# Weight chunks loaded out of order into free ring slots and idle projection buffers, new planned costs for three GpSimd operations, and one tail copy moved to ScalarE

## Chip, cores and metric

One core of one Trainium2 chip. The metric is the device time of one execution in microseconds (us), taken over several executions; the profiles are single executions. The chip can slow TensorE's clock; the share of full speed that it allows is called the granted clock here. The experiments ran on four occasions, each on another chip, and each time the kernel before ran along.

## The reference

Two layers, each of attention (32 heads of 16) and a gated feed-forward network, on a sequence of 2048 with width 512 and F = 1792. The second layer uses the same weights again.

```python
def _A_ref(x, wqkv, wo):                      # H = 32, Dh = 16
    qkv = (x @ wqkv).reshape(B, S, 3, H, Dh).transpose(2, 0, 3, 1, 4)
    q, k, v = qkv[0], qkv[1], qkv[2]
    p = softmax(einsum("bhqd,bhkd->bhqk", q, k) * Dh ** -0.5)
    return einsum("bhqk,bhkd->bhqd", p, v).transpose(0, 2, 1, 3).reshape(B, S, D) @ wo

def _B_ref(x, w_gate, w_up, w_down):
    return (gelu(x @ w_gate) * (x @ w_up)) @ w_down

x = x + _A_ref(layernorm(x), wqkv, wo)        # S = 2048, D = 512
x = x + _B_ref(layernorm(x), w_gate, w_up, w_down)
x = x + _A_ref(layernorm(x), wqkv, wo)        # the same two again
x = x + _B_ref(layernorm(x), w_gate, w_up, w_down)
```

## The kernel before

The attention takes nearly all of the time. TensorE forms the scores, ScalarE exponentiates most tiles (VectorE computes the others with integer arithmetic), TensorE multiplies the result by V. The feed-forward network of a block of 512 rows is fitted in between the attention work of the next block, so only the last half-block of the second layer is left for a tail without attention.

How the order of the instructions comes about: the kernel does not write them down in a fixed order. A planner in Python, run while the kernel is built, records them one by one. It keeps its own clock: each recorded operation has a **planned cost**, and each engine a time at which it is next free.

```python
def op(self, eng, fn, r=(), w=(), grp=None, cost=0.1, lat=0.15, at=0.0):
    start = max(self.free[eng], at, self.ready(eng, r, w))
    # ... dependencies on earlier reads and writes ...
    self.free[eng] = start + cost
    o.seen = start + cost + lat
    return o
```

In each step the main loop compares these planned times, and so decides what comes next on TensorE:

```python
while True:
    t = now[0] = max(now[0], sch.free["pe"])
    pump(t)                        # jobs of VectorE, GpSimd, SP whose planned start is before t
    # ...
    F = fill_ready()
    if F is not None and F <= t + 0.02:
        fill()                     # scores for the next exponential
        continue
    # ...
    if fit >= 1 and (full >= want or full and (rest or press)):
        pv(its, min(fit, full, 6)) # attention times V
        continue
    # ... else a piece of projection or feed-forward work that fits before the limit,
    # ... else keep_clock(): a filler matmul of zeros, added to the accumulator bank
    now[0] = t + 0.05
sch.model = (now[0], log["idle"], dict(sch.free))   # the planned end
```

The program that is built gives every engine its instructions in that order, with waits for what they need, whatever the real durations turn out to be.

The last half-block's weights come in 256 KB chunks, in a ring of slots `WR` and, for that half-block only, in six spare slots in the buffers of the projection weights `WK`, `WV`, `WQ`. Chunks are loaded strictly in order, so a chunk that has to wait holds up all behind it; and the spare slots wait until all projection work (`prep`) has been taken off its list:

```python
wst = {"loaded": 0, "next": 0, "here": set(), "done": set()}
# ...
def wfeed():
    while wst["loaded"] < len(wlist):
        i = wst["loaded"]
        if wlast[i] >= 0 and wlast[i] not in wst["done"] or wslots[i] >= NWR and prep:
            break
        wload()
```

The LayerNorm's reciprocal root is three short GpSimd operations; the last argument of each is its planned cost. Most calls have `n` = 2 or 4 columns, those in the tail `n` = 1:

```python
def ln_scale(n, then, lo=0):
    # ...
    job("pool", 1, [
        (lambda e: e.tensor_scalar(LNS[:, 0, lo:lo + n], var, LN_EPS, None, op0=ALU.add), keys,
         [("LNS", lo + i) for i in range(n)], 0.3),
        (lambda e: e.tensor_tensor(LNS[:, 1, lo:lo + n], LNS[:, 0, lo:lo + n], CM05[:, 0:n], op=ALU.pow),
         [("LNS", lo + i) for i in range(n)] + [("CM05",)], [("LNS", lo + i) for i in range(n)], 1.1),
        (lambda e: e.tensor_scalar(LNS[:, 2, lo:lo + n], mean, -1.0, None, op0=ALU.mult),
         keys + [("LNS", lo + i) for i in range(n)], [("LNS", lo + i) for i in range(n)], 0.3)], then)
```

Of the kernel before, what the change touches and what calls it, by code (L numbers as in the profile page):

```python
# [175 lines left out]
def _emit_fast(nc, es, x_in, wqkv, wo, wg, wu, wd, out, n_rep=2):  # L176
# [12 lines left out]
    NCK = D // 128  # L189
# [3 lines left out]
    NQB = S // 512  # L193
# [15 lines left out]
    def sb(name, shape, dt):  # L209
        return es.enter_context(nc.sbuf_tensor(name, shape, dt))  # L210
# [12 lines left out]
    NWR = 7  # L223
# [4 lines left out]
    CM05 = sb("fCM05", [128, 4], F32)  # L228
# [19 lines left out]
    LNS = sb("fLNS", [128, 3, 8], F32)  # L248
# [20 lines left out]
    def bankbf(b):  # L269
        return PS[:, b, :].bitcast(F16)  # L270
# [3 lines left out]
    def dma(eng, grp, dst, src, r=(), w=(), serial=False, kb=32):  # L274
        if grp not in sch.groups:
            sch.add_dma_group(grp, serial=serial)
        t = max(sch.free[eng], sch.ready(eng, r, w)) + 0.5
        wire[0] = max(t, wire[0]) + kb / 180.0
        return sch.op(eng, lambda e: e.dma_start(dst, src), r=r, w=w, grp=grp, cost=0.5, lat=wire[0] - t + 1.3)
# [101 lines left out]
    wlist = []  # L381
    for layer in range(n_rep):
        for qb in range(NQB):
            halves = layer == n_rep - 1 and qb == NQB - 1 and NQB > 1
            for h in ((0, 1) if halves else (None,)):
# [2 lines left out]
                    w_tail = len(wlist)  # L388
                wlist += [("g", i) for i in range(NFT // 2)] + [("u", i) for i in range(NFT // 2)]
                wlist += [("d", i) for i in range(NFT // 2)]  # L390
    wst = {"loaded": 0, "next": 0, "here": set(), "done": set()}
    NWX = 6 if NQB > 1 else 0
    wslots, wlast = [], {}
    for i in range(len(wlist)):
        k = i - w_tail
        s = NWR + k % (NWR + NWX) if 0 <= k and k % (NWR + NWX) < NWX else None
        if s is None:
            s = i % NWR if k < 0 else (w_tail + k - NWX) % NWR
        wslots.append(s)
        wlast[i] = max([j for j in range(i) if wslots[j] == s], default=-1)  # L400

    def wslot(s):
        if s < NWR:
            return WR[:, s, :]
        W = (WK, WV, WQ)[(s - NWR) // 2]
        return W[:].rearrange("p a b -> p (a b)")[:, 2 * D * ((s - NWR) % 2):2 * D * ((s - NWR) % 2 + 1)]

    def wload():
        i = wst["loaded"]
        wst["loaded"] += 1  # L410
        kind, k = wlist[i]
        s = wslots[i]
        if kind == "d":
            dst = wslot(s)[:, 0:2 * D].rearrange("p (a b) -> p a b", a=2)
            src = wd_src[:, 2 * k:2 * k + 2, :]
        else:
            dst = wslot(s)[:, 0:NCK * 256].rearrange("p (a b) -> p a b", a=NCK)
            src = (wg_src if kind == "g" else wu_src)[:, :, 256 * k:256 * (k + 1)]
        keys = [("WR", s)]
        if s >= NWR:  # L420
            keys += [(("WK", "WV", "WQ")[(s - NWR) // 2], c) for c in range(NCK)]
        job("sp", 1, [(lambda: dma("sp", "wr%d" % s, dst, src, w=keys, serial=True, kb=256), [], keys, None)],
            lambda o: wst["here"].add(i))

    def wfeed():
        while wst["loaded"] < len(wlist):
            i = wst["loaded"]
            if wlast[i] >= 0 and wlast[i] not in wst["done"] or wslots[i] >= NWR and prep:
                break
            wload()  # L430

    def wget(kind, k):
        i = wst["next"]
# [4 lines left out]
    def wdone(i):  # L438
        wst["done"].add(i)
        wfeed()  # L440
# [13 lines left out]
    def job(eng, prio, ops, then=None, ported=False):  # L454

        serial[0] += 1
        jobs[eng].append((prio, serial[0], ops, then, ported or eng == "pool"))
# [51 lines left out]
    have = set()  # L509
# [7 lines left out]
    def give_back(b):  # L517
        if b in lent:
            lent.discard(b)
            slot_open[0 if b in SLOTS[0] else 1] -= 1  # L520
        elif b in held3:
            held3.discard(b)
        else:
            free_banks.add(b)
# [35 lines left out]
    def evac_job(prio, b, ops, then=None):  # L560
        def done(o):
            give_back(b)
            if then is not None:
                then(o)
        dve(prio, ops, done)

    def xn(i, alt):
        return HT[:, i + 4 * alt, 0:D].bitcast(F16)

    def xnkey(i, alt):  # L570
        return ("HT", i + 4 * alt)
# [5 lines left out]
    def ln_scale(n, then, lo=0):  # L577
        keys = [("MV", lo + i) for i in range(n)]
        mean = AP(MV, 2 * lo, [[16, 128], [2, n]])
        var = AP(MV, 2 * lo + 1, [[16, 128], [2, n]])  # L580
        job("pool", 1, [
            (lambda e: e.tensor_scalar(LNS[:, 0, lo:lo + n], var, LN_EPS, None, op0=ALU.add), keys,
             [("LNS", lo + i) for i in range(n)], 0.3),
            (lambda e: e.tensor_tensor(LNS[:, 1, lo:lo + n], LNS[:, 0, lo:lo + n], CM05[:, 0:n], op=ALU.pow),
             [("LNS", lo + i) for i in range(n)] + [("CM05",)], [("LNS", lo + i) for i in range(n)], 1.1),
            (lambda e: e.tensor_scalar(LNS[:, 2, lo:lo + n], mean, -1.0, None, op0=ALU.mult),
             keys + [("LNS", lo + i) for i in range(n)], [("LNS", lo + i) for i in range(n)], 0.3)], then)

    def ln_check(n, lo=0):
        var = AP(MV, 2 * lo + 1, [[16, 128], [2, n]])  # L590
        dve(2, [(lambda e: e.scalar_tensor_tensor(OKV[:, 0:n], var, L_HI, OKV[:, 0:n], op0=ALU.is_le, op1=ALU.mult),
                 [("MV", lo + i) for i in range(n)] + [("OKV",)], [("OKV",)], 0.1)])

    def ln_apply(i, rows, key, eng, alt, then=None, us=None, st=0):
        us = us or (1.05 if eng == "pool" else 0.46)
        job(eng, 1, [(lambda e: e.tensor_scalar(xn(i, alt), rows, LNS[:, 2, st + i:st + i + 1], LNS[:, 1, st + i:st + i + 1],
                                                op0=ALU.add, op1=ALU.mult),
                      [key, ("LNS", st + i)], [xnkey(i, alt)], us)], then, ported=True)

    def transpose_piece(i, tt, alt=False, eng="dve", then=None):  # L600
        def fn(e, bs):
            for ck in range(NCK):
                ins = e.transpose(bankbf(bs[0])[:, ck * 128:(ck + 1) * 128], xn(i, alt)[:, ck * 128:(ck + 1) * 128],
                                  IDN[:, :])
            return ins

        def after(bs):
            b = bs[0]
            dst = XNT[:, :, tt * 128:(tt + 1) * 128]
            src = bankbf(b)[:, 0:NCK * 128].rearrange("p (a b) -> p a b", a=NCK)  # L610
            if eng == "act":
                sch.op("act", lambda e: e.activation(dst, src, ACTF.Copy), r=[BK[b]], w=[("XNT", tt)], cost=0.6)
                give_back(b)
                if then is not None:
                    then(None)
            else:
                evac_job(1, b, [(lambda e: e.tensor_copy(dst, src), [BK[b]], [("XNT", tt)], 0.335)], then)

        return Piece(0.06 * NCK, [xnkey(i, alt), ("IDN",)], fn, after)
# [14 lines left out]
    def got(name):  # L634
        return lambda o: have.add(name)
# [179 lines left out]
    prep = []  # L815
# [175 lines left out]
    def ln_thread(tts, xsl, check, name, eng, step=2):  # L991

        nt = len(tts)

        def scale(lo):
            hi = min(lo + step, nt)

            def apply(o):
                for i in range(lo, hi):
                    ln_apply(i, X[:, xsl[i], :], ("X", xsl[i]), eng, False, got(("xn", name, i)))  # L1000
            ln_scale(hi - lo, apply, lo)
            if check:
                ln_check(hi - lo, lo)

        ready = 0
        for i, tt in enumerate(tts):
            while ("xn", name, i) not in have:
                while ready < nt and all(("st", name, k) in have for k in range(ready, min(ready + step, nt))):
                    scale(ready)
                    ready += step  # L1010
                yield None
            yield transpose_piece(i, tt, then=got(("tr", name, i)))
        while not all(("tr", name, i) in have for i in range(len(tts))):
            yield None

    def post(layer, qb, h):
# [13 lines left out]
        for i, tt in enumerate(tts):  # L1030
            def evac_x(b, i=i, x=xsl[i]):
# [4 lines left out]
                           [("AT", c, k) for c in range(NCK) for k in hs]  # L1036
                           + [("WO",)], evac_x, cols=D)
        yield from ln_thread(tts, xsl, True, (layer, qb, 2, h), "dve" if qb == NQB - 1 else "pool",
                             1 if h == 1 else 2)
        xs = slice(512 * qb + q0, 512 * qb + q0 + qn)  # L1040
# [171 lines left out]
    unit_order = []  # L1212
# [97 lines left out]
    def left():  # L1310
        return cur or nxt[0] < len(segs)
# [327 lines left out]
    while True:  # L1639
# [62 lines left out]
        now[0] = t + 0.05  # L1702
        log["idle"] += 0.05
        assert now[0] < 20000.0, "no progress"
    assert not unit_order and wst["next"] == len(wlist) and not left()
    sch.model = (now[0], log["idle"], dict(sch.free))
    return sch, FLAG

# [855 lines left out]
```

## Time and profile before

| | before |
|---|---|
| time, median of 3 runs | 1644.64 us (1643.25 to 1645.59) |
| span of the profiled run, first to last instruction | 1644.3 us |
| exponentials on ScalarE | 1490.6 us busy, 25.9 us idle before them |
| last attention accumulator begins to be copied (end of the "body") | 1597.1 us |
| output projection starts | 1611.3 us |
| gate matmuls start | 1621.4 us |

First the busy times at the head of the profile of the kernel before (engine, us, share of the span, number of instructions), then its costliest group: line, engine, operation, tiles, count, then busy us and mean ns of one, then idle time ahead of them and what ended most of it.

```profile
span 1644.3 us, 38836 instructions
## 1 busy us (share of the span) xinstructions
PE 1558.4 (95%) x16491; PEld 520.8 (32%) x16491; DVE 1363.4 (83%) x2341; ACT 1566.0 (95%) x1349; POOL 181.3 (11%) x233
...
L1380 ACT ACTIVATE fPT<-fPS 128x1536 bf16<-128x1536 f32 (+1 forms) x1306 | 1490.6, 1282 | 25.9 <-PE fPS L1366 23.0
```

The names of the tiles: `fPS` are the banks that TensorE writes, `fPT` the exponentials, `fOS` a copied accumulator, `fLT` row sums, `fRB` their inverses after the broadcast, `fAT` the normalised attention, `fXNT` and `fHT` inputs and results of the projections and of the feed-forward network.

The waits of ScalarE in the kernel before, between 50 and 1594 us (what waited, for what: us, times, longest):

```profile
ACT fPT L1380 <- PE fPS L1366: 16.3, 50, 1.1
```

The body is thus ScalarE working almost without a pause, fed with scores by TensorE. The tail is another matter. The end of the chain of waits of the kernel before (start us, us, what):

```profile
1597.09 0.44 DVE fOS L930
...
1603.78 6.61 DMA fRB<-rscr
...
1610.52 0.73 POOL fAT L895
1611.30 2.79 PE fPS L626 x8
1614.09 5.60 PE fPS L1532 x45
1619.69 0.33 PE fPS L603 x4
...
1620.35 0.33 PE fPS L603 x4
...
1621.43 11.47 PE fPS L1047 x104
```

The copy of the last accumulator (L930) follows the last attention matmul; the row sums are gathered, inverted and stored (not shown), and come back as a broadcast (`fRB`, 6.61 us); L626 is the output projection; L1532 are clock-keeping fillers; L603 are the two transposes; L1047 the gate matmuls. TensorE stood idle for 2.18 us before the projection, waiting for the broadcast. Windows of the kernel before around it (busy us and count by engine, then granted clock, share of DMA, GB/s):

```profile
1602.00:1612.00 10.00, 7.82 (x97) 3.33 (x96) 1.55 (x4) 0.00 (x0) 0.72 (x1) 1.00 1.03 281
1612.00:1616.00 4.00, 4.00 (x30) 1.26 (x32) 3.37 (x9) 0.00 (x0) 1.18 (x4) 0.57 0.09 25
```

The DMA engines were fully busy (share 1.03) while the broadcast was under way, and the clock was 0.57 in the 4 us after the stall. The SP queue's timeline of the kernel before shows what was loaded shortly ahead (start, us, engine, line, operation, tiles): six gate chunks for the spare buffers `fWK`, `fWV`, `fWQ`, of which three are shown.

```profile
1592.82 0.47 SPq L279 DMA_DIRECT2D fWK<-in_B_w_gate_dram  x1
...
1599.67 0.42 SPq L279 DMA_DIRECT2D fWK<-in_B_w_gate_dram  x1
...
1600.69 0.51 SPq L279 DMA_DIRECT2D fWQ<-in_B_w_gate_dram  x1
```

### The profile page before, as it was taken

What the parts mean: (1) busy time and instruction counts of PE and PEld (TensorE: products, weight loads), DVE (VectorE), ACT (ScalarE), POOL (GpSimd) and SP (SyncE); (2) the same over time, 40 slices, a digit from 0 to 9 for tenths busy, and PEclk for the clock granted to TensorE, in tenths of its full rate; (3) what the DMA queues carried; (4) which work ended last, traced back from release to release, by engine and by line L of the source; (5) the groups of instructions that cost most, each with busy time, mean ns of one, the idle gap of its engine ahead of it and who ended that gap; (6) DMA issues with size and microseconds to landing.
All of it is one profiled execution on the core that took longest, in us unless ns stands there. A gap on an engine that the chain in (4) does not pass through costs nothing.

```text
span 1644.3 us, 38836 instructions
## 1 busy us (share of the span) xinstructions
PE 1558.4 (95%) x16491; PEld 520.8 (32%) x16491; DVE 1363.4 (83%) x2341; ACT 1566.0 (95%) x1349; POOL 181.3 (11%) x233
## 2 busy tenths in 40 slices
PE   8999999999999999999999989999999999999998
PEld 3332222222222223222333322222222222434454
DVE  7889998889988899888643899878899879888883
ACT  6999999999999999999999999999999999999971
POOL 3401020011100210002410100100010000100000
PEclk9999999999999999999999999999999999999999
DMA  5200101123011400214113110111401104121254
GB/s 148 59 9 7 46 21 53 49 71 93 21 49 47 132 23 23 56 38 125 30 52 110 34 51 25 34 49 33 125 21 47 49 22 124 33 70 50 63 150 123
DMA packets 120963, 97.24 MB, mean 59 GB/s; under 512 B 11472, under 2 KB 103888, under 8 KB 120784
## 3 DMA queue, kind: packets, MB, share of 16 engines
q1 hardware_dynamic: 116928, 89.95, 19.3%
q0 software_dynamic: 2112, 4.19, 1.0%
q8 instruction: 134, 2.20, 0.6%
q10 hardware_dynamic: 1744, 0.53, 0.1%
q14 instruction: 45, 0.37, 0.1%
HBM read 76.81 MB, written 15.20 MB: 56 GB/s over the span
## 4 chain that ended last, share of the span: by engine, by line
ACT 58%; PE 29%; DVE 8%; DMA 3%; POOL 1%; issue 1%; SPq 0%; DVEq 0%; POOLq 0%; ACTq 0%
ACT fPT L1380 54%; PE fPS L1366 8%; PE fPS L1512 8%; PE fPS L1047 6%; DVE fPI L1420 3%; PE fPS L1111 3%; DVE fPP L1460 3%; ACT fHT L1329 3%; PE fPS L626 2%; DMA fRB<-rscr 2%; PE fPS L1532 1%; DMA rscr<-fLT 1%; ACT L1329 1%; ACT L1380 1%; POOL fAT L895 1%
## 5 line engine op out<-in xcount | busy, mean ns | idle before, releaser
L1380 ACT ACTIVATE fPT<-fPS 128x1536 bf16<-128x1536 f32 (+1 forms) x1306 | 1490.6, 1282 | 25.9 <-PE fPS L1366 23.0
L1420 DVE TENSOR_SCALAR fPI<-fPS 128x512 int16<-128x512 f32 x831 | 563.9, 684 | 100.9 <-PE fPS L1366 96.1
L1366 PE MATMUL fPS<-fQ,fKT 32*128 32x512 f16 (+1 forms) x4608 | 523.3, 359 | 50.2 <-ACT fPT L1380 36.3
L1512 PE MATMUL fPS<-fPT,fVP 128*17 128x512 bf16 (+1 forms) x3670 | 464.9, 359 | 7.2 <-DVE fOS L930 3.0
L1460 DVE TENSOR_SCALAR fPP<-fPI 128x2048 int16<-128x2048 int16 (+3 forms) x708 | 429.7, 638 | 13.1 <-PE fPS L1512 7.4
L1512 PE MATMUL fPS<-fPP,fVD 128*17 128x512 f16 (+1 forms) x2814 | 405.3, 357 | 5.3 <-DVE fPP L1460 1.7
L1366 PEld LDWEIGHTS fPS<-fQ,fKT 32*128 32x128 f16 x4608 | 140.0, 91 | 521.6 <-ACT fPT L1380 382.5
L1512 PE MATMUL fPS<-fPI,fVP 128*17 128x512 f16 (+1 forms) x938 | 256.7, 357 | 0.4 <-DVE fPP L1460 0.2
L1047 PE MATMUL fPS<-fXNT,fWR 128*128 128x512 f16 (+1 forms) x952 | 219.9, 362 | 7.2 <-DVE fHT L1090 4.7
L1512 PEld LDWEIGHTS fPS<-fPT,fVP 128*17 128x17 f16 x3670 | 118.2, 88 | 156.0 <-issue 94.1
L895 POOL TENSOR_TENSOR fAT<-fOP,fRB 128x512 f16<-128x512 f32 (+1 forms) x36 | 42.6, 1183 | 974.3 <-DMA fRB<-rscr 974.3
L1532 PE MATMUL fPS<-fONB,fZV 128*17 128x512 f16 x1836 | 145.0, 386 | 1.7 <-POOL fQMASK L364 1.5
L1512 PEld LDWEIGHTS fPS<-fPP,fVD 128*17 128x17 f16 x2814 | 109.2, 89 | 107.5 <-issue 45.8
L1111 PE MATMUL fPS<-fWR,fHT 128*128 128x512 bf16 x428 | 117.4, 382 | 0.1
L1047 PEld LDWEIGHTS fPS<-fXNT,fWR 128*128 128x128 bf16 x952 | 76.7, 98 | 112.0 <-issue 19.6
L1090 DVE TENSOR_TENSOR fHT<-fPS,fHT 128x512 bf16<-128x512 f32 x112 | 76.1, 688 | 42.4 <-PE fPS L1047 31.3
L1066 DVE CAST fHT<-fPS 128x512 bf16<-128x512 f32 x105 | 71.6, 686 | 26.9 <-PE fPS L1047 26.7
L1512 PEld LDWEIGHTS fPS<-fPI,fVP 128*17 128x17 f16 x938 | 65.0, 88 | 34.0 <-issue 18.9
L706 POOL TENSOR_SCALAR fVD<-fVP 128x544 f16<-128x544 f16 (+1 forms) x48 | 56.2, 1171 | 130.8 <-DVE fVP L714 128.1
L1532 PEld LDWEIGHTS fPS<-fONB,fZV 128*17 128x17 f16 x1836 | 43.2, 91 | 50.1 <-issue 25.1
L930 DVE COPY fOS<-fPS 128x512 f32<-128x512 f32 (+1 forms) x72 | 45.0, 625 | 11.5 <-PE fPS L1512 11.2
L672 DVE TENSOR_SCALAR fQ<-fPS,fQMASK 128x512 f16<-128x512 f32 (+1 forms) x72 | 46.2, 683 | 3.5 <-PE fPS L626 3.3
(71 smaller groups left out, 663.1 us busy)
## 6 DMA issues: line engine op xcount, KB each, us to landing
fWR<-in_B_w_up_dram SPq DMA_DIRECT2D x62, 256.0 KB, 2.9
fWR<-in_B_w_down_dram SPq DMA_DIRECT2D x58, 256.0 KB, 2.8
fWR<-in_B_w_gate_dram SPq DMA_DIRECT2D x57, 256.0 KB, 4.9
oscr<-fOS SPq DMA_DIRECT2D x224, 32.0 KB, 1.7
fOP<-oscr SPq DMA_DIRECT2D x28, 256.0 KB, 2.6
fRB<-rscr SPq DMA_DIRECT2D x28, 256.0 KB
fX<-in_A_x_dram POOLq DMA_DIRECT2D x4, 1024.0 KB, 5.7
xscr<-fX SPq DMA_DIRECT2D x16, 256.0 KB, 2.8
```

What stands on the lines that cost most here:

```text
L895: job("pool", 1, [(lambda e: e.tensor_tensor(AT[:, c, q0:q0 + qn], OP[:, slot, 0:qn], RB[:, slot, 0:qn], op=ALU.mult), [("OP", slot), ("RB ...
L1047: ins = e.matmul(bank(bs[0])[:, w * qn:(w + 1) * qn], lhsT=wchunk(s, (ft + w) % 2, ck), rhs=XNT[:, ck, xs], start=(ck == 0), stop=(ck == N ...
L1066: evac_job(1, b, [(lambda e: e.tensor_copy(in_ht(ft), in_bank(b)), [BK[b]], fk, 0.6)], got(("gate", layer, qb, h, ft)))
L1090: (lambda e: e.tensor_tensor(in_ht(ft), in_bank(b), in_ht(ft), op=ALU.mult), [BK[b]] + fk, fk, 0.62)], got(("up", layer, qb, h, ft))))
L1111: ins = e.matmul(bank(b)[:, 0:D], lhsT=HT[:, ft, i * 128:(i + 1) * 128], rhs=wslot(s)[:, jj * D:(jj + 1) * D], start=(ft == 0), stop=(ft = ...
L1329: sch.op("act", lambda e, lo=lo, hi=hi: e.activation(HT[:, lo:hi, q0:q0 + qn], HT[:, lo:hi, q0:q0 + qn], ACTF.Gelu_apprx_tanh), r=keys, w= ...
L1366: ins = e.matmul(bank(b)[:, b0:b0 + qn], lhsT=KT[32 * j:32 * j + 32, (x[1] % NG) // 2, kt * 128:(kt + 1) * 128], rhs=Q[32 * j:32 * j + 32, ...
L1380: o = sch.op("act", lambda e: e.activation(PT[:, p, 0:512 * na].rearrange("p (a b) -> p a b", a=na), PS[:, b0:b0 + na, :], ACTF.Exp, scale ...
L1420: dve(0, [(lambda e: e.tensor_scalar(PI[:, gi, 512 * r:512 * (r + 1)], bank(bd), DBIAS, 0.0, op0=ALU.add, op1=ALU.max), [BK[bd]], [("PI", ...
L1460: shifts.append((s, [(lambda e: e.tensor_scalar(PP[:, s, 0:512 * n], PI[:, gi, 0:512 * n], int(OCT) * ph // NPH, None, op0=ALU.add), [("PI ...
L1512: ins = e.matmul(PS[32 * j:32 * j + VW, ACC, 0:qn], lhsT=l, rhs=r_, start=a, stop=z, tile_position=(0, 32 * j), skip_group_check=True)
L1532: ins = e.matmul(PS[32 * j:32 * j + VW, ACC, :], lhsT=ZV[:, :], rhs=ones, start=False, stop=False, tile_position=(0, 32 * j), skip_group_c ...
```

## The change

Its intent is a shorter tail. **Weights:** any chunk whose slot is free may be loaded, in any order, and a spare slot counts as free as soon as the projections that read it are done. **Planned costs:** the three GpSimd operations are planned at 0.25, 0.45 + 0.16 n and 0.25 us in place of 0.3, 1.1 and 0.3, nearer to what they take (the profile has them at 0.23, 0.58 and 0.23 us in the tail). **Copy:** ScalarE, idle by then, copies the first of the two transposed tiles of the tail.

```diff
-    wst = {"loaded": 0, "next": 0, "here": set(), "done": set()}
+    wst = {"waiting": None, "next": 0, "here": set(), "done": set()}
 # ...
+    def wspare(s):
+        kind = ("k", "v", "q")[(s - NWR) // 2]
+        if kind == "q":
+            return not prep
+        return all((n_rep - 1, kind, c, kb) in have for c in range(NCK) for kb in range(NQB))
 # ...
-    def wload():
-        i = wst["loaded"]
-        wst["loaded"] += 1
+    def wload(i):
 # ...
     def wfeed():
-        while wst["loaded"] < len(wlist):
-            i = wst["loaded"]
-            if wlast[i] >= 0 and wlast[i] not in wst["done"] or wslots[i] >= NWR and prep:
-                break
-            wload()
+        if wst["waiting"] is None:
+            wst["waiting"] = list(range(len(wlist)))
+        for i in list(wst["waiting"]):
+            if wlast[i] >= 0 and wlast[i] not in wst["done"] or wslots[i] >= NWR and not wspare(wslots[i]):
+                continue
+            wst["waiting"].remove(i)
+            wload(i)
 # ... in ln_scale, the planned costs of the three operations:
-             [("LNS", lo + i) for i in range(n)], 0.3),
+             [("LNS", lo + i) for i in range(n)], 0.25),
-             [...], [("LNS", lo + i) for i in range(n)], 1.1),
+             [...], [("LNS", lo + i) for i in range(n)], 0.45 + 0.16 * n),
-             keys + [...], [("LNS", lo + i) for i in range(n)], 0.3)], then)
+             keys + [...], [("LNS", lo + i) for i in range(n)], 0.25)], then)
 # ... in ln_thread (step == 1 only in the tail):
-            yield transpose_piece(i, tt, then=got(("tr", name, i)))
+            yield transpose_piece(i, tt, eng="act" if step == 1 and i % 2 == 0 else "dve", then=got(("tr", name, i)))
 # ... and an assertion at the end
```

No arithmetic of the kernel changes. With the change, the same lines stand seven further down: L1373 scores, L1387 exponentials, L1519 attention times V, L1539 fillers, L633 projection, L610 transposes, L1054 gate.

More of the change, by code (lines that the diff above doesn't have):

```diff
@@ L582, in ln_scale @@
             (lambda e: e.tensor_scalar(LNS[:, 0, lo:lo + n], var, LN_EPS, None, op0=ALU.add), keys,
-             [("LNS", lo + i) for i in range(n)], 0.3),
+             [("LNS", lo + i) for i in range(n)], 0.25),
             (lambda e: e.tensor_tensor(LNS[:, 1, lo:lo + n], LNS[:, 0, lo:lo + n], CM05[:, 0:n], op=ALU.pow),
-             [("LNS", lo + i) for i in range(n)] + [("CM05",)], [("LNS", lo + i) for i in range(n)], 1.1),
+             [("LNS", lo + i) for i in range(n)] + [("CM05",)], [("LNS", lo + i) for i in range(n)], 0.45 + 0.16 * n),
             (lambda e: e.tensor_scalar(LNS[:, 2, lo:lo + n], mean, -1.0, None, op0=ALU.mult),
-             keys + [("LNS", lo + i) for i in range(n)], [("LNS", lo + i) for i in range(n)], 0.3)], then)
+             keys + [("LNS", lo + i) for i in range(n)], [("LNS", lo + i) for i in range(n)], 0.25)], then)
     def ln_check(n, lo=0):
@@ L1704, in _emit_fast @@
         assert now[0] < 20000.0, "no progress"
-    assert not unit_order and wst["next"] == len(wlist) and not left()
+    assert not unit_order and wst["next"] == len(wlist) and not wst["waiting"] and not left()
     sch.model = (now[0], log["idle"], dict(sch.free))
```

## The prediction

> **What bounds it now.** The table of engines has ScalarE busy 1566.0 of 1644.3 us. Its exponentials (1490.6 us; 653 of 1536 columns at 1494 ns, 653 of 1024 at 1071 ns) run from 14.9 to 1595.5 us; the waits view finds ScalarE idle only 16.3 us between 50 and 1594. Then comes a tail of 49 us without exponentials (timeline, chain of waits): last accumulator copied 1597.1; row sums gathered (1.9), inverted (0.95), stored (3.3), broadcast back (6.6); output projection at 1611.3 (2.8); 5.6 us of clock-keeping filler matmuls in the chain, though the normalised rows were ready at 1616.4 and 1617.8; transposes 1619.6 and 1620.3; gate from 1621.4; then TensorE runs on to 1640.5.
>
> **What the change does.**
> 1. Weights. The last half-block's six gate chunks for the idle projection buffers were issued at 1592.8 to 1593.9 and 1599.7 to 1600.7. Now four go early in the second layer, two with the previous half's gates. Between 1602 and 1612 the windows show the DMA engines 0.9 to 1.17 busy at 263 to 301 GB/s, and the 128 KB broadcast lands last. The Trainium skill ("Trainium Kernel Development and Optimization", Key Constraints) says that all issuing queues run on the same 16 engines and interleave; the trace agrees: alone on its queue the broadcast took 6.6 us. Three chunks (0.79 MB) fewer at 290 GB/s is, estimated, 2.7 us less.
> 2. Planner costs: the LayerNorm trio on GpSimd is planned at 1.11 us (one column), not 1.7; measured 1.2. Filler changes: 160 instead of 112 before the output projection, then 44 + 32 + 4 instead of 88 + 4 + 12.
> 3. One of two tail transposes is copied by the idle ScalarE (598 ns; VectorE 415 ns).
> 4. The body is re-planned: 652 exponentials of 1536 and 655 of 1024, +0.65 us of ScalarE. The head loses 20 fillers, about -0.15 us.
>
> **Critical path, estimated.** Count from the last attention matmul (1597.0). Before, the projection starts at +14.3. After, 18 down matmuls (0.227 us each, 4.1) and 160 fillers (0.056 each, 9.0) keep TensorE to +13.1, while the broadcast should be in at +10 to +11: the filler becomes the limit, and the gain is 1.2 us, not 2.7. Projection to gate took 10.1. Without the 2.2 us of idleness before it the clock should not drop (0.57 in 1612 to 1616) and the projection takes 1.95; rows ready at +5.0 and +6.4; 44 fillers, transpose to +5.5, 32 fillers (1.8), transpose to +7.6, copy, gate at +8.2: gain 1.9. The tail gains 3.1. The body gives back 0.65, perhaps 0.3 more as more attention matmuls follow the last exponential, and may move 2 us either way by its waits.
>
> **Prediction:** 1641.7 us, 1637.5 to 1645.0 with 8 in 10. Faster by over 2%: 0.01; within 2%: 0.98; slower: 0.01.
>
> **To look for.** No load into the projection buffers between 1592 and 1601; the broadcast landing in 4 to 5 us; no TensorE idleness before the output projection, filler instead of the broadcast in the chain; clock 1.0 there; projection to gate 8.2 us; gate to end unchanged (23 us); last exponential within 2 us of 1595.5; exponentials busy 1491.2 us.
>
> **What would make it wrong.** A body gaining or losing more than 2 us in ScalarE waits, which no view of before shows; the up chunks, issued earlier now, colliding with row-sum store and broadcast as the gate chunks did, so that it lands after +13; filler slower than 0.056.

## The result, and the profile after

| | before | after |
|---|---|---|
| time, median of 4 runs each | 1644.41 us (1643.25 to 1645.59) | 1652.92 us (1650.97 to 1653.94) |
| span of the profiled run | 1644.3 us | 1650.3 us |
| exponentials: busy, idle before them | 1490.6, 25.9 us | 1492.5, 33.7 us |
| last accumulator begins to be copied | 1597.1 us | 1606.9 us |
| from there to the output projection | 14.2 us | 12.6 us |
| projection to gate | 10.1 us | 7.9 us |
| gate to the end | 22.9 us | 22.9 us |

(The last three rows are read from the timeline, in which the projection of the kernel after starts at 1619.51; the chain shown below has it at 1619.58.)

The ratio is 1.005, with a 95% interval of 1.0033 to 1.0068. Ratios here are the mean time of one kernel's runs over that of the other's of the same rounds, so not quite the ratio of the medians. The change is within 2%, but it is a loss, and 1652.9 lies far above the predicted range of 1637.5 to 1645.0.

The head of the page of the kernel after, and its exponentials:

```profile
span 1650.3 us, 38750 instructions
## 1 busy us (share of the span) xinstructions
PE 1559.9 (95%) x16441; PEld 521.8 (32%) x16441; DVE 1362.6 (83%) x2336; ACT 1568.5 (95%) x1351; POOL 176.6 (11%) x233
...
L1387 ACT ACTIVATE fPT<-fPS 128x1536 bf16<-128x1536 f32 (+1 forms) x1307 | 1492.5, 1279 | 33.7 <-PE fPS L1373 29.9
```

The waits of ScalarE of the kernel after, between 50 and 1594 us:

```profile
ACT fPT L1387 <- PE fPS L1373: 23.5, 59, 2.0
```

ScalarE is busy 1.9 us longer and idle 7.8 us longer in the exponentials, and the time is lost in the body: the last accumulator is 9.8 us later. In this profile the tail did what was asked of it. The end of the chain of the kernel after:

```profile
1605.86 0.98 PE fPS L1519 x20
1606.85 3.99 PE fPS L1118 x18
1610.84 8.74 PE fPS L1539 x160
1619.58 0.98 PE fPS L633 x4
...
1624.63 1.84 PE fPS L1539 x32
...
1627.40 11.53 PE fPS L1054 x104
```

No broadcast stands in it: the down matmuls (L1118) and 160 fillers lead straight to the projection, 12.7 us after the last attention matmul (1606.85 to 1619.58), and the gate starts 7.8 us later (1627.40). The window of the kernel after that corresponds to the saturated one (columns as before):

```profile
1610.00:1620.00 10.00, 10.00 (x167) 4.44 (x166) 1.30 (x4) 0.00 (x0) 0.73 (x1) 1.00 0.86 239
```

The SP queue's timeline of the kernel after, its loads of gate chunks into the spare buffers late in the second layer:

```profile
1544.78 0.40 SPq L279 DMA_DIRECT2D fWQ<-in_B_w_gate_dram  x1
...
1548.33 0.37 SPq L279 DMA_DIRECT2D fWQ<-in_B_w_gate_dram  x1
```

The clock is 1.00, TensorE has no gap, and the gate chunks come 48 us and more ahead of where they were. (The other four spare chunks are loaded far earlier still, at 1033 to 1037 us.)

One piece of the 9.8 us can be seen by itself. In the body of this profile there is a stall; the chain of the kernel after around it:

```profile
1401.45 5.68 DMA fRB<-rscr
...
1407.27 1.38 POOL fAT L902
...
1408.69 1.04 PE fPS L633 x4
```

The window of the kernel after just behind it:

```profile
1410.00:1415.00 5.00, 5.00 (x69) 1.84 (x64) 2.74 (x5) 2.69 (x3) 0.00 (x0) 0.66 0.02 5
```

TensorE stood at L633 for 1.98 us, for a broadcast of 5.68 us that took 3.99 us in the kernel before; then the clock was 0.66 for a window, and ScalarE waited twice for about 2 us. In the second profile of the same kernel (`e5_after_again`, below) the stall is 0.10 us and the clock there 1.00. So this is a chance of the one run, not a property of the change. It is a warning against explaining a difference by the largest wait that one trace shows.

### The profile page after: what moved, and what is told of

The parts are those of the page before. It is cut to its first block, busy times and chain, and to the rows that moved or that the text cites. A ratio compares the mean times of both kernels' runs of the same rounds, so it can differ in the third digit from the quotient of the medians. Undisturbed runs are those within 1.5% of the kernel's fastest.

```text
span 1650.3 us, 38750 instructions
## 1 busy us (share of the span) xinstructions
PE 1559.9 (95%) x16441; PEld 521.8 (32%) x16441; DVE 1362.6 (83%) x2336; ACT 1568.5 (95%) x1351; POOL 176.6 (11%) x233
## 3 DMA queue, kind: packets, MB, share of 16 engines
q8 instruction: 133, 2.18, 0.6%
## 4 chain that ended last, share of the span: by engine, by line
ACT 60%; PE 31%; DVE 6%; DMA 1%; issue 1%; POOL 1%; SPq 0%; DVEq 0%; POOLq 0%
ACT fPT L1387 57%; PE fPS L1373 9%; PE fPS L1519 8%; PE fPS L1054 7%; PE fPS L633 3%; ACT fHT L1336 2%; PE fPS L1118 2%; DVE fPI L1427 2%; DVE fPP L1467 2%; PE fPS L1539 1%; DMA fRB<-rscr 1%; ACT L1336 1%; PE fPS L700 1%; DVE fHT L1073 0%; ACT L1387 0%
## 5 line engine op out<-in xcount | busy, mean ns | idle before, releaser
L1387 ACT ACTIVATE fPT<-fPS 128x1536 bf16<-128x1536 f32 (+1 forms) x1307 | 1492.5, 1279 | 33.7 <-PE fPS L1373 29.9
L1373 PE MATMUL fPS<-fQ,fKT 32*128 32x512 f16 (+1 forms) x4608 | 528.7, 359 | 57.5 <-ACT fPT L1387 43.2
L1519 PE MATMUL fPS<-fPT,fVP 128*17 128x512 bf16 (+1 forms) x3676 | 463.1, 359 | 8.2 <-DVE fOS L937 3.8
L1519 PE MATMUL fPS<-fPP,fVD 128*17 128x512 f16 (+1 forms) x2796 | 394.1, 359 | 2.2 <-POOL fVD L713 0.9
L1373 PEld LDWEIGHTS fPS<-fQ,fKT 32*128 32x128 f16 x4608 | 142.8, 91 | 535.2 <-ACT fPT L1387 385.0
L1519 PE MATMUL fPS<-fPI,fVP 128*17 128x512 f16 (+1 forms) x932 | 256.1, 359 | 1.7 <-DVE fOS L937 1.0
L1054 PE MATMUL fPS<-fXNT,fWR 128*128 128x512 f16 (+1 forms) x952 | 219.5, 362 | 6.3 <-DVE fHT L1097 4.6
L1519 PEld LDWEIGHTS fPS<-fPT,fVP 128*17 128x17 f16 x3676 | 117.9, 88 | 151.3 <-issue 89.9
L1539 PE MATMUL fPS<-fONB,fZV 128*17 128x512 f16 x1804 | 143.3, 387 | 1.7 <-POOL fQMASK L364 1.5
L1519 PEld LDWEIGHTS fPS<-fPP,fVD 128*17 128x17 f16 x2796 | 107.0, 89 | 103.4 <-issue 48.5
L1118 PE MATMUL fPS<-fWR,fHT 128*128 128x512 bf16 x428 | 118.2, 383 | 0.5 <-DVE fQ L679 0.3
L1054 PEld LDWEIGHTS fPS<-fXNT,fWR 128*128 128x128 bf16 x952 | 77.0, 97 | 111.8 <-issue 21.6
L1519 PEld LDWEIGHTS fPS<-fPI,fVP 128*17 128x17 f16 x932 | 64.0, 88 | 36.1 <-issue 19.0
L1539 PEld LDWEIGHTS fPS<-fONB,fZV 128*17 128x17 f16 x1804 | 42.1, 91 | 47.8 <-issue 24.4
```

The source lines that it names most:

```text
L1054: ins = e.matmul(bank(bs[0])[:, w * qn:(w + 1) * qn], lhsT=wchunk(s, (ft + w) % 2, ck), rhs=XNT[:, ck, xs], start=(ck == 0), stop=(ck == N ...
L1118: ins = e.matmul(bank(b)[:, 0:D], lhsT=HT[:, ft, i * 128:(i + 1) * 128], rhs=wslot(s)[:, jj * D:(jj + 1) * D], start=(ft == 0), stop=(ft = ...
L1373: ins = e.matmul(bank(b)[:, b0:b0 + qn], lhsT=KT[32 * j:32 * j + 32, (x[1] % NG) // 2, kt * 128:(kt + 1) * 128], rhs=Q[32 * j:32 * j + 32, ...
L1387: o = sch.op("act", lambda e: e.activation(PT[:, p, 0:512 * na].rearrange("p (a b) -> p a b", a=na), PS[:, b0:b0 + na, :], ACTF.Exp, scale ...
L1519: ins = e.matmul(PS[32 * j:32 * j + VW, ACC, 0:qn], lhsT=l, rhs=r_, start=a, stop=z, tile_position=(0, 32 * j), skip_group_check=True)
L1539: ins = e.matmul(PS[32 * j:32 * j + VW, ACC, :], lhsT=ZV[:, :], rhs=ones, start=False, stop=False, tile_position=(0, 32 * j), skip_group_c ...
```

## The experiments

The recorded orders were compared. With the **weights part alone**, the records of ScalarE, VectorE and GpSimd are the same as before, and TensorE's differs in the last 96 of its 3686 planner entries only. With the **copy alone**, TensorE's record is the same to the end. With the **costs alone**, the record of the body is the same as the full change's, and differs from before's from the first microseconds on. So three lines of planned costs re-draw the whole body; nothing else in the change touches the order of the compute engines there (the weights part moves loads in SyncE's record).

Three theories:

- **A:** the re-drawn order is worse by itself. A planner that decides by comparing planned times is thrown onto another course by any small change of a cost; the kernel before is a good draw among many, and the change is an average one.
- **B:** the weight loads, now out of order and among the attention work, disturb the body.
- **C:** the new costs are too optimistic, so TensorE comes to its matmuls too early and stalls.

### The parts alone, and two small variations

`e1_weights`: the weights part alone (costs and copy as before).

> The weight part alone (out of order, spare buffers), old planner costs, copy on VectorE. The planner that records the schedule ends its own clock at 1618.0 us here, 1619.6 for before and 1623.5 for the change; the chip took 24.8 and 29.4 us longer than those. Theory A (the loss is the luck of a re-drawn schedule, whichever part re-draws it; the chip follows the plan, plus up to 5 us of waits that the plan doesn't see): 1641 to 1648 us. Theory B (weight loads moved earlier disturb the body): 1650 to 1655 us, most of the 8.5 us loss, with more ScalarE waits between 1350 and 1480 us. Theory C (the shorter planned LayerNorm costs make the plan too optimistic and TensorE stalls in order): no loss, 1641 to 1645.

`e2_costs`: the planned costs alone.

```diff
-             [("LNS", lo + i) for i in range(n)], 0.3),
+             [("LNS", lo + i) for i in range(n)], 0.25),
-             [...], [("LNS", lo + i) for i in range(n)], 1.1),
+             [...], [("LNS", lo + i) for i in range(n)], 0.45 + 0.16 * n),
-             keys + [...], 0.3)], then)
+             keys + [...], 0.25)], then)
```

> The planned costs of the LayerNorm trio alone. The planner's clock ends at 1631.9 us, 12.3 later than for before. Theory A: slow in proportion, 1654 to 1662 us, with ScalarE waits or fewer tiles for VectorE spread where the plan lost them. Theory B: 1642 to 1646, since no load moves. Theory C: 1650 to 1655, with new TensorE waits for LayerNorm results (GpSimd, normalised rows).

`e3_null111`: the kernel before with one cost changed by a hundredth, an edit that means nothing.

```diff
-             [...], [("LNS", lo + i) for i in range(n)], 1.1),
+             [...], [("LNS", lo + i) for i in range(n)], 1.11),
```

> Before with one planner number moved by 0.01 us (the power operation planned at 1.11 instead of 1.10, further from what it takes), an edit with no purpose. The planner's clock ends at 1623.1 us, 3.5 later. Theory A: 1646 to 1652 us, a loss like the change's own from nothing. Theories B and C: 1643 to 1646, as before.

`e4_after047`: the full change with the constant moved by 0.02, which gives yet another order, one that the planner's clock thinks as short as before's.

```diff
-             [...], [("LNS", lo + i) for i in range(n)], 0.45 + 0.16 * n),
+             [...], [("LNS", lo + i) for i in range(n)], 0.47 + 0.16 * n),
```

> The whole change with one planner number moved by 0.02 us (0.47 instead of 0.45 in the power operation's planned cost). The planner's clock ends at 1618.1 us, 5.4 earlier than for the change. Theory A: 1641 to 1648, so that most of the loss is gone while every part of the change is there. Theories B and C: 1650 to 1655, as the change.

Measured, against 1645.89 us for the kernel before in the same rounds: `e1_weights` 1646.56 (ratio 0.9998, 0.9975 to 1.0020); `e2_costs` 1659.05 (1.0077, 1.0055 to 1.0098); `e3_null111` 1648.25 (1.0019, 0.9995 to 1.0043); `e4_after047` 1648.03 (1.0011, 0.9984 to 1.0038).

B falls: with all of the new loads and the old order there is no loss. C falls too: `e4_after047` has costs as optimistic as the change's to 0.02 us, and no loss that the interval shows. The costs alone lose most, but part of that is the tail. The chain of `e2_costs`:

```profile
1605.57 3.56 PE fPS L1111 x16
1609.13 15.87 PE fPS L1532 x292
1625.00 0.98 PE fPS L626 x4
```

The projection waits behind 292 fillers, though its input (`fAT`) was begun at 1617.9: that order plans the broadcast late, and TensorE does as planned. The tail is 51.4 us long here and 47.2 before. The body alone is 7.2 us longer than in the first profile of before (last accumulator at 1604.3).

### The change again; only the tail's costs; the copy alone

`e5_after_again`: the change unaltered (a comment added), on another occasion.

> The change unaltered, once more. Its planner ends 3.9 us later than before's; in the first comparison the chip lost 8.5. If the other 4.6 us belong to the change (the stall of 2 us at 1407 us behind the late broadcast, and the clock of 0.66 after it), the loss is again 7 to 10 us and the profile shows the stall and a ScalarE wait of about 2 us near 1410 and 1415. If they were luck of those runs, the loss is 3 to 6 us and the stall is under 1 us.

`e6_tail_costs_act`: the new costs only where `n` is 1, which leaves the body's order alone, and the copy.

```diff
-             [...], [("LNS", lo + i) for i in range(n)], 1.1),
+             [...], [("LNS", lo + i) for i in range(n)], 0.61 if n == 1 else 1.1),
 # ... 0.25 if n == 1 else 0.3 for the other two
-            yield transpose_piece(i, tt, then=got(("tr", name, i)))
+            yield transpose_piece(i, tt, eng="act" if step == 1 and i % 2 == 0 else "dve", then=got(("tr", name, i)))
```

> Old order of weight loads; new planned costs only where one column is normalised (the last half-block alone), and the copy on ScalarE, so that every engine's record is the same as before's until the last LayerNorm. Theory A: the body of before, and only the filler between output projection and gate shrinks: projection to gate 8 to 9 us instead of 10.1, total 0.5 to 2.5 us faster than before (1642 to 1645). Theory C (optimistic costs stall TensorE): not faster.

`e7_weights_tail_costs_act`: the same with the weights part, that is, the whole change without its effect on the body. It was built to beat both kernels.

> The whole change, except that the new planned costs hold only for one column. The records of ScalarE, VectorE and GpSimd are those of before until the last LayerNorm, and TensorE's until the last 96 of its 3686 entries. Theory A: body of before and tail of the change, from last accumulator to the end 43.5 to 44.5 us instead of 47.2: 2.5 to 4 us faster than before, 1640.5 to 1643.5 on the chip of the first comparison. Theory B (earlier loads disturb the body): slower than the run without them by over 3 us.

`e8_act`: the copy alone.

> The ScalarE copy alone. TensorE's record is that of before to the end. The second transpose, which VectorE copies in both, lands last, so projection to gate stays 10.1 us and the total within 1 us of before. If the copy matters by itself, the gate starts 0.3 to 0.5 us earlier.

Measured, against 1647.71 us: `e5_after_again` 1650.76 (1.0032, 1.0015 to 1.0050); `e6_tail_costs_act` 1647.05 (0.9995, 0.9981 to 1.0008); `e7_weights_tail_costs_act` 1645.53 (0.9992, 0.9979 to 1.0006); `e8_act` 1644.99 (0.9985, 0.9973 to 0.9997).

The loss of the change repeats, at 5.3 us by its ratio. In the second profile the exponentials of `e5_after_again` read:

```profile
L1387 ACT ACTIVATE fPT<-fPS 128x1536 bf16<-128x1536 f32 (+1 forms) x1307 | 1492.4, 1275 | 29.8 <-PE fPS L1373 26.1
```

Busy time as in the first, idle time 3.9 us less: that much of the waits was chance. Without the re-drawn body, the loss is gone (`e6`, `e7`). But `e7` missed its expectation of a gain of 2.5 to 4 us. Its chain shows why:

```profile
1604.11 6.25 DMA fRB<-rscr
...
1610.50 0.73 POOL fAT L902
...
1611.28 3.23 PE fPS L633 x8
1614.50 2.79 PE fPS L1539 x44
```

The broadcast took 6.25 us with the gate chunks long since loaded, against 6.61 before; TensorE stalled for 1.99 us ahead of the projection and took 3.23 us for it. In this run the early gate chunks did not clear the way for the broadcast. The seeming gain of `e8_act`, whose TensorE record is before's, is one of nine comparisons up to then; `e6`, `e7` and, in the next group, `e10_weights_act` contain the same copy and show no such gain. Two more expectations were missed: `e6` did not gain its 0.5 to 2.5 us, and in `e8_act` projection to gate took 8.4 us, not 10.1. The copy is not shown to be the reason: in `e12_before_pad57` (below), which has before's order and before's copy, it took 8.2 us. The 10.1 us of the first profile of before contain the slowed clock that followed its stall.

### Another draw, and the time outside the span

`e9_after042`: the full change with another constant, again an order that the plan thinks as short as before's. (The text on record counts 28 different schedules among the settings; a later count came to 19, and no output of either is kept, so neither is used.)

```diff
-             [...], [("LNS", lo + i) for i in range(n)], 0.45 + 0.16 * n),
+             [...], [("LNS", lo + i) for i in range(n)], 0.42 + 0.16 * n),
```

> The whole change with its planned power operation at 0.42 + 0.16 n instead of 0.45 + 0.16 n: of 84 such settings (28 different schedules, planner's ends 1618.7 to 1630.0, median 1623.5, so the change's own 1623.5 is the middle) the one with the earliest last accumulator, 1577.1 on the planner's clock against 1576.6 for before and 1581.8 for the change. Theory A: body of before, tail of the change (43 to 45 us): 0 to 4 us faster than before in the same rounds, last accumulator near 1600 us. If the parts of the change cost anything in themselves: as slow as the change, over 3 us slower than before.

`e10_weights_act`: the weights part and the copy, with the old costs.

> Both tail parts without the new planned costs: records of ScalarE, VectorE, GpSimd as before until the tail. Theory A: body of before; tail about 44.5 us as in the weights-alone run against 44.5 to 47.2 in profiles with before's own tail: 0 to 3 us faster than before.

By then a second thing had shown. The device time exceeds the span by 1.7 to 1.9 us in every run of the kernel before, and by 3.35 to 3.65 us in every run of the change. The two that had it, the change and `e2_costs`, had 5184 and 5185 VectorE instructions in the built program (waits included); the kernel before has 5192, and the others that were counted then had 5190 to 5212. Two kernels test that.

`e11_after_pad8`: the change with eight VectorE stores of one element at the start, planned at no cost, so that the order stays and the count is 5192 as before. `e12_before_pad57`: before with 57, which makes 5249, one above a multiple of 64, as 5185 is.

```diff
+    PAD = sb("fPAD", [1, 64], F32)
 # ...
+    for i in range(8):          # 57 in e12_before_pad57
+        sch.op("dve", lambda e, i=i: e.memset(PAD[:, i:i + 1], 0.0), w=[("PAD", i)], cost=0.0, lat=0.0)
```

> The change plus 8 writes of 4 bytes on VectorE while it waits for the first input. The time outside the traced span (device time minus span) was 1.7 to 1.9 us in every run of six kernels, but 3.2 to 3.9 us in every run of the change and of the planned costs alone. The program of those two has 5184 and 5185 VectorE instructions, all others 5191 or more. If VectorE's instruction count sets the extra 1.7 us, it is gone here (1.6 to 2.0 outside the span) and the total drops by 1.7; if not, it stays at 3.2 to 3.9.

> Before plus 57 such writes, 5249 VectorE instructions, which is 1 above a multiple of 64 as 5185 is (and 5184 is 0 above one). If being just above a multiple of 64 instructions costs the extra, 3.2 to 3.9 us lie outside the span here; if it is the count below 5190 or something else, 1.7 to 1.9.

Measured, against 1646.64 us: `e9_after042` 1646.81 (0.9999, 0.9985 to 1.0013); `e10_weights_act` 1648.42 (1.0004, 0.9990 to 1.0018); `e11_after_pad8` 1652.33 (1.0037, 1.0022 to 1.0052); `e12_before_pad57` 1648.52 (1.0010, 0.9995 to 1.0026).

`e9_after042` is the second order of the full change that loses nothing. The gains that were hoped for, up to 4 us in `e9_after042` and up to 3 in `e10_weights_act`, did not appear. In `e11_after_pad8` the time outside the span fell to 1.74 to 1.86 us: the extra is gone with the schedule unchanged, so it hangs on what was added, eight VectorE instructions and the small tile that they write, and not on the schedule. In `e12_before_pad57` it stayed at 1.7 to 1.9 us, so the rule of 64 is wrong, and what about the count does it stays open. The total of `e11_after_pad8` did not come down, though: its spans were 1.6 us longer than the other runs' of the change (1650.8 against 1649.2 and 1648.5 on average), which is within their scatter. That removing the extra makes the kernel faster is therefore not shown.

### A bad draw on purpose

`e13_after060`: the full change with a constant for which the planner's clock shows a much later end. Theory A says that this is enough to make it slow; B and C have no reason for it, C least of all, because the costs are less optimistic.

```diff
-             [...], [("LNS", lo + i) for i in range(n)], 0.45 + 0.16 * n),
+             [...], [("LNS", lo + i) for i in range(n)], 0.6 + 0.16 * n),
```

> The whole change with the power operation planned at 0.60 + 0.16 n: the latest of the 84 settings on the planner's clock, last accumulator 1588.2 (before 1576.6, the change 1581.8), end 1630.0. Theory A (the chip follows the drawn schedule): last accumulator at 1609 to 1613 us in the profile, against a mean of 1599.7 in seven profiles with before's body and 1604.4 in four with the change's body, tail 43 to 45 us, total 9 to 14 us slower than before, including 1.7 us outside the span because VectorE has 5185 instructions as in the planned-costs run. If the loss belonged to the parts of the change and not to the draw: 5 to 8 us slower, as the change. If the count does not matter: 1.7 to 1.9 us outside the span.

Measured: 1657.43 (1656.51 to 1661.71) against 1645.33, ratio 1.0079 (1.0057 to 1.0101), 12.1 us more by the medians. Its exponentials:

```profile
L1387 ACT ACTIVATE fPT<-fPS 128x1536 bf16<-128x1536 f32 (+1 forms) x1307 | 1493.6, 1279 | 36.6 <-PE fPS L1373 32.5
```

The idle time is 10.7 us above that of the first profile of before, 8.3 above the mean of the seven profiles with before's order (28.3). A's expectation of 9 to 14 us was met. Of the 12.1 us, about 1.9 lie outside the span (its count is 5185, its time outside 3.6 to 3.8 us).

### All runs together

The planner's clock is a model and its absolute times are wrong by 25 us. But the differences in it can be set against the spans of all runs. Planned and measured are differences from the kernel before (planned: last accumulator 1576.6, end 1619.6; measured: mean span of 34 runs 1644.5, last accumulator 1599.7, the mean of the seven profiles with its body order).

| kernel | planned last accumulator | planned end | last accumulator in its profile | mean span, runs |
|---|---|---|---|---|
| the change | +5.2 | +3.9 | +7.2, +2.8, +4.0 | +4.3, 10 |
| `e2_costs` | +5.2 | +12.3 | +4.6 | +10.9, 4 |
| `e13_after060` | +11.6 | +10.4 | +10.2 | +10.1, 4 |
| `e11_after_pad8`, the change's order | +5.2 | +3.9 | +4.0 | +6.3, 4 |
| `e3_null111` | +3.5 | +3.5 | +1.8 | +2.8, 4 |
| `e9_after042` | +0.5 | -0.9 | +2.5 | +0.7, 5 |
| `e4_after047` | -0.2 | -1.5 | +1.6 | +1.5, 4 |
| `e1_weights` | 0.0 | -1.6 | +2.9 | +0.4, 4 |
| `e6_tail_costs_act` | 0.0 | -1.0 | +2.0 | +0.3, 6 |
| `e10_weights_act` | 0.0 | -1.6 | +0.2 | +0.9, 5 |
| `e8_act` | 0.0 | 0.0 | -1.0 | -1.5, 6 |
| `e12_before_pad57`, before's order | 0.0 | 0.0 | +0.1 | +2.2, 4 |
| `e7_weights_tail_costs_act` | 0.0 | -2.7 | -1.8 | -0.5, 6 |

(The +4.3 is from the 4 runs of the first comparison and the 6 of `e5_after_again`, the three profiles are those two and `e11_after_pad8`; with the four runs of the latter +4.3 would be +4.9.) The last column pools all occasions. Against the kernel before in the same rounds, `e13_after060` is +11.4, `e5_after_again` alone +3.6, and no other row moves by more than 0.6. Where the plan is later by 3 us or more, the chip is later by about as much (for `e3_null111` taken alone, the interval of the ratio still includes no loss); where it says up to 2.7 us earlier, the chip shows nothing that stands out from the scatter. One kernel's runs scatter by a standard deviation of 2.1 us (the 34 of before), so the rows from `e9_after042` down cannot safely be told from zero, and this includes the +2.2 of `e12_before_pad57`, whose order is before's.

The plan was also drawn, without running, for 84 settings of the change's constants: ends from 1618.7 to 1630.0, median 1623.5. The change's own 1623.5 is the median. For the kernel before, 1.10 has the neighbours 1.09 with a planned end of 1624.9 and 1.11 with 1623.1. Of 41 values of before's constant from 0.90 to 1.30, its own 1.10 has the earliest planned end (1619.6; the others 1621.7 to 1635.9), and of 41 values in place of the change's 0.45, from 0.30 to 0.70, the median end is again 1623.5 and 36 end later than before.

## Why the prediction was wrong

**The step that failed** is this one: "The body gives back 0.65, perhaps 0.3 more as more attention matmuls follow the last exponential, and may move 2 us either way by its waits." It treats the re-drawn order as a fresh draw around the old one. But the kernel before is a favourable draw, by the planned ends above; a fresh one is on average worse. (That it was picked by tuning is likely.) The prediction's last paragraph names waits of ScalarE in the body as a risk; what it had wrong was to centre them on zero and to allow them 2 us. The runs show it in the body, with before's order at 1599.7 on average and the change's at 1604.4 (four profiles: 1606.9, 1602.5, 1603.7 and 1604.3, the last from `e2_costs`): +4.7 with a standard error of 1.2, planned +5.2. In those profiles the waits of ScalarE are 3.2 us longer (31.5 against 28.3 on average), and the exponentials are busy for 1.7 us longer (1492.5 against about 1490.8), which the prediction had put at 0.65. So the last exponential ended at 1605.4 in the first profile of the change, where it was looked for within 2 us of 1595.5.

The first profile of before, from which the prediction counted, was also a favourable execution of its order. In five of the seven profiles with that order TensorE stands for 1.8 to 2.3 us near 566 us, waiting for normalised rows from GpSimd; their last accumulators come at 1598.7 to 1602.6. In the two without this stall, the first of before and `e7`, they come at 1597.1 and 1597.9.

**The sum.** Over all runs the change takes 6.0 us more (means 1652.3 of 10 runs, 1646.3 of 34). Of this 1.7 lies outside the span (3.5 against 1.8), a term that the prediction did not have at all. The other 4.3, with a standard error of 0.9, is the span: body +4.7, tail -1.8, which makes +2.9; the difference of 1.4 is not resolved by four and seven profiles. The first comparison's 8.5 us between the medians is more than 6.0 because the kernel before ran 1.9 us under its own mean in those rounds, and the change 0.7 us above its; that is within the scatter. (The 1.7 us outside the span are a difference that was measured; the control without them, `e11_after_pad8`, was no faster in total.)

**The tail: right in its mechanism in this profile, smaller on average.** The steps came as predicted: the projection after 12.7 us (13.1 predicted), limited by the filler and not by the broadcast; no idleness of TensorE, clock 1.0; projection to gate 7.8 us (8.2); gate to end unchanged at 22.9 us; loads into spare buffers gone from the crowded stretch. The broadcast, from its issue to the start of the product that it releases, took 5.2 us in this profile, 5.8 and 6.8 in the two others of the same order; 4 to 5 was predicted, so this held at best once. The filler hid the 5.8; the 6.8, in `e11_after_pad8`, came too late, and TensorE stood for 1.51 us before the projection: there the broadcast was the limit again. Against the first profile of before the tail gained 3.7 us (47.2 to 43.5), 3.1 predicted. But before's tail in that profile was a long one. Its record ran twice more with the same TensorE order (`e8_act`, 44.5; `e12_before_pad57`, 46.0), and the change's twice more (43.6, 45.1): on average 45.9 against 44.1, a gain of 1.8. Projection to gate, from which the prediction took 1.9 us, took 8.4 and 8.2 us in these two runs of before's order against 7.7 to 7.9 with the change's: most of that gain was the slow clock of the one profile that the prediction counted from.

**The skill on the DMA engines.** The prediction rested on the Trainium skill ("Trainium Kernel Development and Optimization", Key Constraints), that all issuing queues run on the same 16 engines and interleave; "DMA: Bandwidth & Descriptors" (the paragraph "Arbitration") adds that each engine takes turns between queues packet by packet. The traces agree in direction: DMA share 1.03 with 6.7 us from the broadcast's issue to its product before, 0.86 with 5.2 us after. Over all profiles the same stretch took 6.3 us on average in the six without the weights part (5.5 to 6.7) and 5.4 in the nine with it (2.9 to 6.8). So the early chunks seem to be worth about 0.9 us there (standard error 0.4; 0.5 without the one profile at 2.9), and not in every run; the orders differ in other ways too. The estimate of 2.7 us, which let three chunks' bytes translate fully into the broadcast's delay, was too large by a factor of about three.

**The skill on the clock.** "TensorE: Matmul & The Clock Gate" (Part 1) says that the clock is halved after an idle window of about 3.4 us, and that this window is free-running, so that it is a matter of phase. The second half fits, though no run tests the phase itself: a stall of 2.18 us before the projection was followed by a window at 0.57 in the first profile of before, one of 1.98 us by 0.66 in the body of the change, while in `e6_tail_costs_act` a stall of 1.91 us was followed by a projection-to-gate time of 7.9 us, that of an undisturbed run. The length of the stall does not decide it: near 566 us one of 1.80 us was followed by a clock of 0.50 in `e1_weights`, and one of 2.08 us by 1.00 in `e10_weights_act`. The first half does not fit: none of these stalls is as long as 3.4 us. The measurement decides: here a stall of 2 us can cost the clock and need not.

**What stays open.** Why this order feeds ScalarE worse: no single stage could be named; in the second profile of the change the longest of 57 waits of ScalarE between 50 and 1590 us is 0.8 us, so the excess is spread over many. What it is about 5184 and 5185 VectorE instructions that adds 1.7 us outside the span. And no version was found to beat the kernel before beyond the scatter; the best candidate, `e7`, is at 0.9992 (0.9979 to 1.0006).

## What to carry to other kernels

When a program's order comes from a planner, a changed cost is not a local edit: it draws a new schedule for everything, and if the kernel at hand is a good draw, as here, expect a loss of the size of the spread between draws and look at that spread (neighbouring constants, an edit that means nothing) before crediting or blaming the idea. To try an idea for one stage, confine its costs to that stage, so that the rest of the record can be shown to be unchanged. And compare more than one profile of each kernel before naming a wait as the cause: the largest wait in the first trace here was gone in the second.

## What the Trainium skill lacked or had wrong

- No page tells of time outside the span that changes with the number of VectorE instructions: 3.2 to 3.9 us in all runs of the programs with 5184 or 5185 of them (the change on two occasions, `e2_costs`, `e13_after060`), 1.7 to 2.0 us in all runs of the other programs (5190 to 5249 where counted), and back to 1.74 to 1.86 us when eight were added to the change. (The nearest page is "Runtime: NRT & Kernel Launch", section "Instruction fetch mechanics"; no run here tests whether what it describes is the cause.)
- "TensorE: Matmul & The Clock Gate", Part 1, gives an idle window of about 3.4 us for the clock to fall. Here stalls of 2.18 and 1.98 us were followed by windows of 4 to 5 us at 0.57 and 0.66 on average, and one of 1.80 us by 0.50 for about 3 us, while stalls of 1.91 and 2.08 us were followed by a clock of 1.00.
- "DMA: Bandwidth & Descriptors" tells how the engines share, not what a small transfer loses by it. Here one and the same broadcast of the body took 3.99 us in one profile and 5.68 in another, and that of the tail, from issue to the product that it releases, 2.9 to 6.8 us over fifteen profiles beside varying weight loads.
- No page gives the scatter of one program's runs: a standard deviation of 2.1 us on 1644.5 us over 34 runs, in which a change of 0.1% cannot be seen with four or five runs.
